# A decode step of gated attention and a squared-ReLU FFN: FFN, wo and q products placed ahead of the V-products in TensorE's order, and one maximum placed ahead of another pair's V-products

## The chip, the core and the metric

The kernel runs on one core of a Trainium2 chip. The metric is the device time of one execution in microseconds (us), and less is better. Five engines take part, each with an instruction stream of its own that it works through strictly in order: TensorE (PE in the profile, with its weight loads as PEld), VectorE (DVE), ScalarE (ACT), GpSimd (POOL) and SyncE (SP). SP computes nothing here; it issues nearly all the loads from HBM, and an issue that has to wait holds up the issues behind it. All loads of SP go out on one DMA queue (q1).

## What is computed

One token of decoding for a batch of two. The result mixes an attention block over a cache of 4096 positions (16 heads of 256) with an FFN, with a gate per batch row:

```python
def _A_ref(x, k_cache, v_cache, wq, wo):
    q = (x @ wq).reshape(B, Sq, H, Dh).transpose(0, 2, 1, 3)
    scores = jnp.einsum("bhqd,bhkd->bhqk", q, k_cache) * (Dh ** -0.5)
    p = _softmax(scores, axis=-1)
    o = jnp.einsum("bhqk,bhkd->bhqd", p, v_cache)
    return o.transpose(0, 2, 1, 3).reshape(B, Sq, H * Dh) @ wo

def _B_ref(x, w1, b1, w2, b2):
    h = jnp.einsum("bsd,df->bsf", x, w1) + b1
    r = jnp.where(h > 0, h, 0)
    return jnp.einsum("bsf,fd->bsd", r * r, w2) + b2

g = _sigmoid((x * gate_w).sum(-1, keepdims=True))
return g * _A_ref(x, ...) + (1 - g) * _B_ref(x, ...)
```

x is [2, 1, 448], K and V are [2, 16, 4096, 256] each, wq is [448, 4096], wo is [4096, 448], w1 is [448, 1792] and w2 is [1792, 448], all float32.

## The kernel before

The 32 pairs of a batch row b and a head h are numbered i = 2h + b. Each pair has one K tile and one V tile of 128 partitions x 8192 floats (4096 KB). In the tile names of the program k0_3 is the K tile of b = 0, h = 3, which is pair 6; the profile leaves the numbers out and writes k and v.

**The ring.** All big loads share one pool of five such tiles (`RING`, line 54; `slot`, line 68): wq, w1, w2 in two parts, four groups of wo, and every K and V. A load may be issued once the tile that stood in its buffer was read for the last time. SP issues in the order of the code: in iteration i of the loop at line 351 the K of pair i+1, then the V of pair i, then what else falls due there: w1 at i = 2, the first half of w2 at i = 4, a group of wo at every h % 4 = 2 with b = 1 (i = 5, 13, 21, 29), the second half of w2 at the last pair. At i = 29 (`last - 2`) the K of pairs 30 and 31 are issued together; the last V comes in three pieces.

**The order.** `tc.manual_schedule()` (line 66) keeps each engine's instructions in the order of the code. For pair i the loop runs:

- `maximum(i)` (line 281): DVE takes the maximum m of a row of scores, PE transposes and spreads it (mt, line 285);
- `times_q(i+1, ...)` (line 268): DVE multiplies the next pair's K by q in place, in two pieces around `softmax(i)`, whose first step nb (line 291, DVE) reads mt, and whose exponential p is on ACT (line 294);
- for b = 1, `sums` (PE, line 299) and `norm` (DVE, line 304 onward);
- `values(i)` (line 311): PE multiplies p with V, 16 products of two passes each into po_buf;
- behind it on PE, when it falls due: the spreading of q for later heads (`make_q`, line 218), `turn(h)` (line 320: ACT copies po_buf, PE transposes it to ot, ACT writes oT), the wo products (`project`, line 333), the FFN's first layer with its transposition (`ffn_hidden`, line 232, i = 3) and the first seven w2 products (line 397, i = 5);
- the rest of `times_q(i+1)` and the row sums of pair i+1 (`row_sums`, line 275), both DVE; and at i = 3, behind these, `ffn_square` (line 251), DVE's bias, ReLU and square, which reads the transposed hidden layer pt out of PSUM.

So a V that lands late holds up, on PE, all that stands behind `values(i)`, the next pair's mt among it. At the end, `late` (line 338) adds the last w2 and wo products into fin, ACT copies it to y4 and two small DMAs write the result.

Of the kernel before, what the change touches and what calls it, by code (L numbers as in the profile page):

```python
# [8 lines left out]
F32 = mybir.dt.float32  # L9
# [7 lines left out]
def kernel(  # L17
# [14 lines left out]
    nc = tc.nc  # L32
    P = 128
    B, H, S, DH = k_cache.shape
    D = x.shape[-1]
    F = w1.shape[1]
# [6 lines left out]
    J = 32  # L43
    NCH = NK // J
    HG = 4
    NG = H // HG
# [5 lines left out]
    QH = QB // DH  # L52
    DQ = D // 4
    RING = 5
    WH = FC // 2
    LEAD = 4
    LEAD2 = 16
# [56 lines left out]
    def load_wo(g):  # L114
        t = slot(f"wo{g}")
        tv = t[:, :HG * NJ * D].rearrange("p (h k) -> p h k", h=HG)
        nc.sync.dma_start(tv, wo_v[:, g * HG:(g + 1) * HG, :])
        wo_sb[g] = tv.rearrange("p h (j n) -> p h j n", j=NJ)
# [99 lines left out]
    def make_q(b, n):  # L218

        a, gq = divmod(n, 4)  # L220
        r = 32 * gq + b
        pq = ps.tile([P, 512], F32, name=f"pq{b}_{n}", tag="pq")
        nc.tensor.matmul(pq, ident[:, r:r + 1].to_broadcast([P, P]), qs[:, a, :], start=True, stop=True)  # L223
        t = work.tile([P, QB], F32, name=f"q{b}_{n}", tag=f"q{b}")
        nc.scalar.activation(t, pq, AF.Copy)  # L225
        for k in range(QH):
            q_sb[b, n * QH + k] = t[:, k * DH:(k + 1) * DH]


    hT = const.tile([P, FC, B], F32, name="hT")  # L230

    def ffn_hidden():
        h_sb = const.tile([B, F], F32, name="h_sb")
        ph = ps.tile([P, 512], F32, name="ph", tag="pq")
        for c in range(CF + 1):
            for n in range(FB):
                if c < CF:
                    lt, rhs = xT[:, c, :], w1_t[c][:, n * D:(n + 1) * D]
                else:
                    half, m = divmod(n, FB // 2)  # L240
                    lt, rhs = xT[:, CF + half, :], w1_t[c][:, m * D:(m + 1) * D]
                nc.tensor.matmul(ph[32 * n:32 * n + B, :D], lt, rhs, start=(c == 0), stop=(c == CF))  # L242
        for n in range(FB):
            nc.scalar.activation(h_sb[:, n * D:(n + 1) * D], ph[32 * n:32 * n + B, :D], AF.Copy)  # L244
        hv = h_sb.rearrange("b (p c) -> b c p", c=FC)
        pt = ps.tile([P, FC, B], F32, name="pt", tag="sm")
        for c in range(FC):
            nc.tensor.matmul(pt[:, c, :], hv[:, c, :], ident[:B, :B], start=True, stop=True)  # L248
        return pt
# [31 lines left out]
    def maximum(i):  # L281
        m = work.tile([P, 1], F32, name=f"m{i}", tag="m")
        nc.vector.tensor_reduce(m, s_t[i], axis=AX.X, op=ALU.max)  # L283
        mt = ps.tile([P, 512], F32, name=f"mt{i}", tag="sm")
        nc.tensor.matmul(mt[:, :P], m.to_broadcast([P, P]), ident, start=True, stop=True)  # L285
        return mt
# [10 lines left out]
    def sums(h):  # L297
        sm = ps.tile([P, 512], F32, name=f"sum{h}", tag="sm")
        nc.tensor.matmul(sm[:, :B], ones_pp, rs_t[h], start=True, stop=True)  # L299
        return sm  # L300

    def norm(h, sm):
        rc = work.tile([P, B], F32, name=f"rc{h}", tag="rc")
        nc.vector.reciprocal(rc, sm[:, :B])
        nc.vector.tensor_mul(rc, rc, gP[:, 0, :])
        rl = work.tile([P, B, 2], F32, name=f"rl{h}", tag="rl")
        nc.vector.tensor_tensor(rl, m4.rearrange("p (b s) -> p b s", s=2), rc.unsqueeze(2).to_broadcast([P, B, 2]),
                                op=ALU.mult)
        rl_t[h] = rl

    def values(i, vt):
        b, h = pairs[i]
        po = po_bufs[h % 2]
        for m in range(NK // 2):
            r = 32 * (m % 4)
            j = 2 * m
            nc.tensor.matmul(po[r:r + 4, :], p4[b][:, m, :], vt[j // J][:, j % J:j % J + 2, :].rearrange("p j d -> p (j d)"),  # L317
                             start=(b == 0 and m < 4), stop=(b == B - 1 and m >= NK // 2 - 4))
# [14 lines left out]
    def project(h):  # L333
        for j in range(NJ):
            nc.tensor.matmul(acc[:, :D], oT[h][:, j, :], wo_sb[h // HG][:, h % HG, j, :], start=False,  # L335
                             stop=(h == H - 2 and j == NJ - 1))

    def late(lt, rhs, start=False, stop=False):
        for k in range(4):
            nc.tensor.matmul(fin[32 * k:32 * k + B, :DQ], lt, rhs[:, k * DQ:(k + 1) * DQ], start=start, stop=stop)  # L340
# [6 lines left out]
    for n in range(NCH):  # L347
        times_q(0, n * J, (n + 1) * J)
        row_sums(0, n * J, (n + 1) * J)
    sm = None  # L350
    for i, (b, h) in enumerate(pairs):

        for n in (range(i + 1, i + 2) if i < last - 2 else range(i + 1, last + 1) if i == last - 2 else ()):
            kts[n] = load_kv(k_cache, n, "k")
        vt = load_kv(v_cache, i, "v", (J // 2, 3 * J // 4) if i == last else ())
        if i == 2:
            load_w1()
        if i == 4:
            load_w2_early()
        if h % HG == HG - 2 and b == B - 1:  # L360
            load_wo(h // HG)
        if i == last:
            load_w2_late()

        mt = maximum(i)
        if i < last:
            times_q(i + 1, 0, LEAD)
        softmax(i, mt)
        if i < last:
            times_q(i + 1, LEAD, LEAD2)  # L370
        if b == B - 1:
            norm(h, sums(h))
        if i == last - 1:

            for hh in range(H - HG, H - 1):
                project(hh)
            ya = const.tile([B, D], F32, name="ya")
            nc.scalar.activation(ya, acc[:, :D], AF.Copy)
            late(ident[:B, :B], ya, start=True)
        values(i, vt)  # L380
        if b == 0 and h % QH == QH - 1 and h + 1 < H:
            make_q(0, (h + 1) // QH)
        if b == 1 and h % QH == QH - 1 and h + 1 < H:
            make_q(1, (h + 1) // QH)
        if b == B - 1:
            turn(h)
        if h % HG == HG - 1 and h < H - 1:
            if b == 0:
                for hh in range(h - HG + 1, h):
                    project(hh)  # L390
            else:
                project(h)
        if i == 3:
            pt = ffn_hidden()
        if i == 5:
            for c in range(WH):
                nc.tensor.matmul(acc[:, :D], hT[:, c, :], w2_sb[c], start=False, stop=False)
        if i < last:
            times_q(i + 1, LEAD2, J)
            row_sums(i + 1, 0, J)  # L400
            for n in range(1, NCH):
                times_q(i + 1, n * J, (n + 1) * J)
                row_sums(i + 1, n * J, (n + 1) * J)
        if i == 3:
            ffn_square(pt)

    for c in range(WH, FC - 2):
# [37 lines left out]
```

## Time and profile before

| | |
|---|---|
| median of three runs | 697.7 us (696.03 to 698.03) |
| the profiled execution | 695.98 us, its span 694.2 us |
| VectorE busy | 583.4 us (84%), 260 instructions |
| ScalarE busy | 41.3 us (6%) |
| GpSimd busy | 0.7 us |
| granted TensorE clock, mean | 0.683 |

The span runs from the first to the last instruction of the program; 1.8 us of the execution lie around it. Busy time is a mean over stages, and the stages of this kernel differ only at three places: the start (about 30 us until the first K has landed), pairs 3 to 7, where the FFN is worked in, and the end from pair 29 on. In between, the same pattern of two loads to a pair repeats. The rows that carry the argument stand in the prediction.

### The profile page before, as it was taken

The page shows a single profiled execution, that of the slowest core. Times are in us where ns is not written, and L with a number is a line of the kernel's source. Part 1 is how long each engine was busy: PE and PEld are TensorE (multiplying, and loading weights), DVE is VectorE, ACT ScalarE, POOL GpSimd, SP SyncE. Part 2 cuts the span into 40 slices and gives each one's busy share as a digit, 9 for nine tenths or more (in the row PEclk, how much of TensorE's full clock was granted, in tenths as well). Part 3 has the DMA queues.
Part 4 walks back from the last instruction along what each step waited for, and adds up shares of the span by engine and source line. Part 5 has one row for each costly group of instructions (what it writes and reads, how often), then busy time and mean ns, then how long its engine had stood idle before and what let it go on. Part 6 is the DMA issues. An engine that isn't in the chain of part 4 may idle for free.

```text
span 694.2 us, 3854 instructions
## 1 busy us (share of the span) xinstructions
PE 296.8 (43%) x1570; PEld 89.3 (13%) x1570; DVE 583.4 (84%) x260; ACT 41.3 (6%) x123; POOL 0.7 (0%) x6
## 2 busy tenths in 40 slices
PE   4312443737165344432276344332465433344265
PEld 1000110502011010100111011010111001011012
DVE  2299988299969998999689999999689999999781
ACT  0200000100000000000000000000000000000000
POOL 0000000000000000000000000000000000000000
PEclk9756665757576666766577755766568665665597
DMA  9999999998899999999999999999999999999992
GB/s 369 448 423 437 434 427 425 426 441 363 334 448 426 425 446 424 427 436 425 424 440 431 426 440 427 431 430 417 438 433 434 429 432 430 436 427 430 429 416 116
DMA packets 13100, 289.79 MB, mean 417 GB/s; under 512 B 1430, under 2 KB 1436, under 8 KB 3868
## 3 DMA queue, kind: packets, MB, share of 16 engines
q1 hardware_dynamic: 12920, 289.54, 97.4%
q8 instruction: 12, 0.20, 0.1%
q10 hardware_dynamic: 164, 0.02, 0.0%
q14 instruction: 4, 0.03, 0.0%
HBM read 289.56 MB, written 0.00 MB: 417 GB/s over the span
## 4 chain that ended last, share of the span: by engine, by line
DMA 57%; DVE 31%; PE 9%; ACT 1%; issue 1%; SPq 0%; DVEq 0%; ACTq 0%
DMA k<-in_A_k_cache_dram 32%; DMA v<-in_A_v_cache_dram 25%; DVE s L279 15%; DVE k L273 15%; PE po_buf L317 5%; PE pt L248 1%; PE ot L329 1%; PE acc L335 1%; PE pq L223 1%; ACT o L323 0%; PE mt L285 0%; PE ph L242 0%; DVE nb L291 0%; ACT q L225 0%; ACT h_sb L244 0%
## 5 line engine op out<-in xcount | busy, mean ns | idle before, releaser
L273 DVE TENSOR_TENSOR k<-k,q 128x3072 f32<-128x3072 f32 (+3 forms) x94 | 286.0, 3057 | 60.1 <-DMA k<-in_A_k_cache_dram 60.0
L317 PE MATMUL po_buf<-v,p 128*4 128x512 f32 x1024 | 180.8, 870 | 234.5 <-DMA v<-in_A_v_cache_dram 232.5
L279 DVE TENSOR_REDUCE s<-k 128x32 f32<-128x8192 f32 x32 | 277.9, 8686 | 2.2
L317 PEld LDWEIGHTS po_buf<-v,p 128*4 128x4 f32 x1024 | 30.1, 109 | 359.5 <-issue 253.2
L285 PE MATMUL mt<-ident,m 128*128 128x128 f32 x64 | 19.5, 395 | 96.6 <-DVE m L283 96.5
L294 ACT ACTIVATE p<-s,nb 128x32 f32<-128x32 f32 x32 | 10.4, 324 | 288.8 <-DVE nb L291 288.8
L285 PEld LDWEIGHTS mt<-ident,m 128*128 128x128 f32 x64 | 12.4, 241 | 115.5 <-issue 92.6
L335 PE MATMUL acc<-wo,oT 128*2 128x448 f32 x60 | 24.3, 550 | 0.8 <-ACT oT L331 0.8
L329 PE MATMUL ot<-rl,o 128*128 128x2 f32 x128 | 17.7, 260 | 14.8 <-ACT o L323 14.8
L299 PE MATMUL sum<-rs,ones_pp 128*128 128x2 f32 x32 | 8.4, 331 | 34.8 <-ACT p L294 34.8
L225 ACT ACTIVATE q<-pq 128x512 f32<-128x512 f32 x16 | 9.6, 597 | 200.9 <-PE pq L223 200.9
L291 DVE TENSOR_REDUCE nb<-mt 128x1 f32<-128x128 f32 x32 | 9.1, 285 | 13.2 <-PE mt L285 13.1
L329 PEld LDWEIGHTS ot<-rl,o 128*128 128x128 f32 x128 | 16.3, 196 | 29.0 <-ACT o L323 29.0
L223 PE MATMUL pq<-qs,ident 128*128 128x512 f32 x32 | 17.7, 641 | 0.0
L323 ACT ACTIVATE o<-po_buf 128x512 f32<-128x512 f32 x16 | 9.5, 595 | 112.0 <-PE po_buf L317 112.0
L299 PEld LDWEIGHTS sum<-rs,ones_pp 128*128 128x128 f32 x32 | 7.0, 273 | 38.4 <-ACT p L294 38.4
L253 DVE TENSOR_TENSOR hb<-pt,b1T 128x28 f32<-128x28 f32 x1 | 0.2, 188 | 13.5 <-PE pt L248 13.5
L248 PE MATMUL pt<-ident,h_sb 2*128 2x2 f32 x28 | 7.0, 378 | 2.3 <-ACT h_sb L244 2.3
L248 PEld LDWEIGHTS pt<-ident,h_sb 2*128 2x128 f32 x28 | 6.9, 336 | 3.1 <-ACT h_sb L244 3.1
L283 DVE TENSOR_REDUCE m<-s 128x1 f32<-128x32 f32 x32 | 5.9, 186 | 1.1
L223 PEld LDWEIGHTS pq<-qs,ident 128*128 128x128 f32 x32 | 4.8, 187 | 14.6 <-issue 13.7
L335 PEld LDWEIGHTS acc<-wo,oT 128*2 128x2 f32 x60 | 4.5, 84 | 16.8 <-issue 15.7
(58 smaller groups left out, 61.2 us busy)
## 6 DMA issues: line engine op xcount, KB each, us to landing
k<-in_A_k_cache_dram SPq DMA_DIRECT2D x32, 4096.0 KB, 25.0
v<-in_A_v_cache_dram SPq DMA_DIRECT2D x31, 4096.0 KB, 30.8
wo<-in_A_wo_dram SPq DMA_DIRECT2D x4, 1792.0 KB, 34.2
wqa<-in_A_wq_dram SPq DMA_DIRECT2D x1, 4096.0 KB, 12.4
wqb<-in_A_wq_dram SPq DMA_DIRECT2D x1, 2048.0 KB, 16.9
v<-in_A_v_cache_dram SPq DMA_DIRECT2D x1, 2048.0 KB, 20.3
v<-in_A_v_cache_dram SPq DMA_DIRECT2D x2, 1024.0 KB, 22.4
w<-in_B_w_dram SPq DMA_DIRECT2D x1, 1792.0 KB, 28.4
```

The lines of the kernel that those rows point to most:

```text
L223: nc.tensor.matmul(pq, ident[:, r:r + 1].to_broadcast([P, P]), qs[:, a, :], start=True, stop=True)
L225: nc.scalar.activation(t, pq, AF.Copy)
L248: nc.tensor.matmul(pt[:, c, :], hv[:, c, :], ident[:B, :B], start=True, stop=True)
L273: nc.vector.tensor_tensor(kt, kt, q_sb[b, h].unsqueeze(1).to_broadcast([P, e - a, DH]), op=ALU.mult)
L279: nc.vector.tensor_reduce(s_t[i][:, n * J + a:n * J + e], kts[i][n][:, a:e, :], axis=AX.X, op=ALU.add)
L285: nc.tensor.matmul(mt[:, :P], m.to_broadcast([P, P]), ident, start=True, stop=True)
L294: nc.scalar.activation(p4[b][:, :, 2 * b:2 * b + 2], s_t[i].rearrange("p (m s) -> p m s", s=2), AF.Exp, bias=nb, accum_out=rs_t[h][:, b:b ...
L299: nc.tensor.matmul(sm[:, :B], ones_pp, rs_t[h], start=True, stop=True)
L317: nc.tensor.matmul(po[r:r + 4, :], p4[b][:, m, :], vt[j // J][:, j % J:j % J + 2, :].rearrange("p j d -> p (j d)"), start=(b == 0 and m < ...
L323: nc.scalar.activation(o, po, AF.Copy)
L329: nc.tensor.matmul(ptv[:, j, :], ov[:, s, j, :], rl_t[h][:, :, s], start=(s == 0), stop=(s == 1))
L335: nc.tensor.matmul(acc[:, :D], oT[h][:, j, :], wo_sb[h // HG][:, h % HG, j, :], start=False, stop=(h == H - 2 and j == NJ - 1))
```

## The change

The change removes no product and no byte; it places work differently.

1. `ffn_hidden` is cut in three. The products with w1 stay at i = 3, but stand ahead of `values(3)`; the transposition (`ffn_turn`) is at i = 4 ahead of `values(4)`; `ffn_square` on DVE follows the row sums at the end of i = 4 instead of i = 3.
2. The seven w2 products of i = 5, and each `make_q`, stand ahead of `values` of the same pair.
3. The wo groups 0 to 2 are loaded two pairs later (i = 7, 15, 23), and their eight products all stand ahead of `values` at i = 8, 16, 24.
4. At i = 29 the row sums and the maximum of pair 30 are written ahead of `values(29)`; on DVE that changes no order, on PE mt of pair 30 stands ahead.

```diff
--- before.py
+++ after.py
@@ -229,8 +229,9 @@
 
     hT = const.tile([P, FC, B], F32, name="hT")
 
+    h_sb = const.tile([B, F], F32, name="h_sb")
+
     def ffn_hidden():
-        h_sb = const.tile([B, F], F32, name="h_sb")
         ph = ps.tile([P, 512], F32, name="ph", tag="pq")
         for c in range(CF + 1):
             for n in range(FB):
@@ -242,6 +243,8 @@
                 nc.tensor.matmul(ph[32 * n:32 * n + B, :D], lt, rhs, start=(c == 0), stop=(c == CF))
         for n in range(FB):
             nc.scalar.activation(h_sb[:, n * D:(n + 1) * D], ph[32 * n:32 * n + B, :D], AF.Copy)
+
+    def ffn_turn():
         hv = h_sb.rearrange("b (p c) -> b c p", c=FC)
         pt = ps.tile([P, FC, B], F32, name="pt", tag="sm")
         for c in range(FC):
@@ -347,7 +350,14 @@
     for n in range(NCH):
         times_q(0, n * J, (n + 1) * J)
         row_sums(0, n * J, (n + 1) * J)
-    sm = None
+
+    def rest(i):
+        times_q(i, LEAD2, J)
+        row_sums(i, 0, J)
+        for n in range(1, NCH):
+            times_q(i, n * J, (n + 1) * J)
+            row_sums(i, n * J, (n + 1) * J)
+
     for i, (b, h) in enumerate(pairs):
 
         for n in (range(i + 1, i + 2) if i < last - 2 else range(i + 1, last + 1) if i == last - 2 else ()):
@@ -357,12 +367,14 @@
             load_w1()
         if i == 4:
             load_w2_early()
-        if h % HG == HG - 2 and b == B - 1:
-            load_wo(h // HG)
+        grp = h // HG
+        if b == B - 1 and h == (H - 2 if grp == NG - 1 else grp * HG + HG - 1):
+            load_wo(grp)
         if i == last:
             load_w2_late()
 
-        mt = maximum(i)
+        if i != last - 1:
+            mt = maximum(i)
         if i < last:
             times_q(i + 1, 0, LEAD)
         softmax(i, mt)
@@ -370,6 +382,20 @@
             times_q(i + 1, LEAD, LEAD2)
         if b == B - 1:
             norm(h, sums(h))
+
+
+        if h % QH == QH - 1 and h + 1 < H:
+            make_q(b, (h + 1) // QH)
+        if h % HG == 0 and b == 0 and h > 0:
+            for hh in range(h - HG, h):
+                project(hh)
+        if i == 3:
+            ffn_hidden()
+        if i == 4:
+            pt = ffn_turn()
+        if i == 5:
+            for c in range(WH):
+                nc.tensor.matmul(acc[:, :D], hT[:, c, :], w2_sb[c], start=False, stop=False)
         if i == last - 1:
 
             for hh in range(H - HG, H - 1):
@@ -377,31 +403,16 @@
             ya = const.tile([B, D], F32, name="ya")
             nc.scalar.activation(ya, acc[:, :D], AF.Copy)
             late(ident[:B, :B], ya, start=True)
+
+        if i == last - 2:
+            rest(i + 1)
+            mt = maximum(i + 1)
         values(i, vt)
-        if b == 0 and h % QH == QH - 1 and h + 1 < H:
-            make_q(0, (h + 1) // QH)
-        if b == 1 and h % QH == QH - 1 and h + 1 < H:
-            make_q(1, (h + 1) // QH)
         if b == B - 1:
             turn(h)
-        if h % HG == HG - 1 and h < H - 1:
-            if b == 0:
-                for hh in range(h - HG + 1, h):
-                    project(hh)
-            else:
-                project(h)
-        if i == 3:
-            pt = ffn_hidden()
-        if i == 5:
-            for c in range(WH):
-                nc.tensor.matmul(acc[:, :D], hT[:, c, :], w2_sb[c], start=False, stop=False)
-        if i < last:
-            times_q(i + 1, LEAD2, J)
-            row_sums(i + 1, 0, J)
-            for n in range(1, NCH):
-                times_q(i + 1, n * J, (n + 1) * J)
-                row_sums(i + 1, n * J, (n + 1) * J)
-        if i == 3:
+        if i < last and i != last - 2:
+            rest(i + 1)
+        if i == 4:
             ffn_square(pt)
 
     for c in range(WH, FC - 2):
```

The first place is PE's order from the V-products of pair 3 on (v1_1; po_buf holds two heads' sums), with ph the FFN's first layer, pt its transposition, w2 the products with the first half of w2, and ot, mt and sum as above. Before:

```order
L317 MATMUL po_buf1_94<-v1_1_0_306,p4_1_101 4x512 x16
L223 MATMUL pq1_1_340<-qs_133,ident_85 128x512
L329 MATMUL ot1_346<-rl1_322,o1_344 128x2 x4
L242 MATMUL ph_354<-w1_267,xT_114 2x448 x16
L248 MATMUL pt_375<-ident_85,h_sb_353 128x2 x14
L285 MATMUL mt4_406<-ident_85,m4_404 128x128
L317 MATMUL po_buf0_92<-v0_2_0_400,p4_0_99 4x512 x16
L285 MATMUL mt5_441<-ident_85,m5_439 128x128
L299 MATMUL sum2_448<-rs2_411,ones_pp_90 128x2
L317 MATMUL po_buf0_92<-v1_2_0_435,p4_1_101 4x512 x16
L329 MATMUL ot2_473<-rl2_453,o2_471 128x2 x4
L397 MATMUL acc_96<-w2_0_402,hT_134 2x448 x7
```

And now:

```order
L223 MATMUL pq1_1_325<-qs_133,ident_85 128x512
L243 MATMUL ph_329<-w1_268,xT_114 2x448 x16
L320 MATMUL po_buf1_94<-v1_1_0_307,p4_1_101 4x512 x16
L332 MATMUL ot1_368<-rl1_323,o1_366 128x2 x4
L288 MATMUL mt4_386<-ident_85,m4_384 128x128
L251 MATMUL pt_394<-ident_85,h_sb_135 128x2 x14
L320 MATMUL po_buf0_92<-v0_2_0_380,p4_0_99 4x512 x16
L288 MATMUL mt5_439<-ident_85,m5_437 128x128
L302 MATMUL sum2_446<-rs2_391,ones_pp_90 128x2
L398 MATMUL acc_96<-w2_0_382,hT_134 2x448 x7
L320 MATMUL po_buf0_92<-v1_2_0_435,p4_1_101 4x512 x16
L332 MATMUL ot2_478<-rl2_451,o2_476 128x2 x4
```

pq and ph now precede the V-products of pair 3, pt (14 transpositions) those of pair 4, and w2 those of pair 5 (v1_2). The row sum of the softmax (sum2) stays ahead of w2.

The second place is SP's order of loads from the first half of w2 on. What a load waits for stands behind it: an engine's name is the one that last read the buffer, and a DMAHW name is an earlier load's semaphore (DMAHW1 to DMAHW4 are here K of pair 4, V of pair 3, K of pair 5 and V of pair 4; DMAHW6, and 7 and 0 in the first rows, are w1, and from the V of pair 6 on DMAHW6 is K of pair 6). Before:

```order
L104 DMA w2_0_402<-in_B_w2_dram 128x3136 [waits DMAHW1_49,DVE_49]
L128 DMA k0_3_0_433<-in_A_k_cache_dram 128x8192 [waits DMAHW6_49,DMAHW2_49,PE_49]
L128 DMA v1_2_0_435<-in_A_v_cache_dram 128x8192 [waits DMAHW7_49,DMAHW0_49,PE_49]
L117 DMA wo0_437<-in_A_wo_dram 128x4x896 [waits DMAHW4_49,PE_49]
L128 DMA k1_3_0_490<-in_A_k_cache_dram 128x8192 [waits DMAHW3_49,DVE_49]
L128 DMA v0_3_0_492<-in_A_v_cache_dram 128x8192 [waits DMAHW6_49,DVE_49]
L128 DMA k0_4_0_533<-in_A_k_cache_dram 128x8192 [waits DMAHW7_49,PE_49]
L128 DMA v1_3_0_535<-in_A_v_cache_dram 128x8192 [waits DMAHW5_49,PE_49]
```

And now:

```order
L104 DMA w2_0_382<-in_B_w2_dram 128x3136 [waits DMAHW6_49,DMAHW7_49,DMAHW0_49,PE_49]
L128 DMA k0_3_0_433<-in_A_k_cache_dram 128x8192 [waits DMAHW1_49,DVE_49]
L128 DMA v1_2_0_435<-in_A_v_cache_dram 128x8192 [waits DMAHW2_49,PE_49]
L128 DMA k1_3_0_488<-in_A_k_cache_dram 128x8192 [waits DMAHW3_49,DVE_49]
L128 DMA v0_3_0_490<-in_A_v_cache_dram 128x8192 [waits DMAHW4_49,PE_49]
L128 DMA k0_4_0_525<-in_A_k_cache_dram 128x8192 [waits DMAHW5_49,PE_49]
L128 DMA v1_3_0_527<-in_A_v_cache_dram 128x8192 [waits DMAHW7_49,PE_49]
L117 DMA wo0_529<-in_A_wo_dram 128x4x896 [waits DMAHW6_49,DVE_49]
```

The w2 load takes the buffer of w1, freed by PE, instead of that of a K, freed by DVE. The V of pair 6 (v0_3) took the buffer of K of pair 6, which DVE's row sums free; it now takes that of V of pair 4, which PE frees. The wo load stands behind the V of pair 7 instead of ahead of the K of pair 7.

The third place is PE's order at pairs 29 and 30 (v1_14 is the V of pair 29). Before:

```order
L285 MATMUL mt29_1500<-ident_85,m29_1498 128x128
L299 MATMUL sum14_1507<-rs14_1468,ones_pp_90 128x2
L317 MATMUL po_buf0_92<-v1_14_0_1494,p4_1_101 4x512 x16
L329 MATMUL ot14_1532<-rl14_1512,o14_1530 128x2 x4
L285 MATMUL mt30_1546<-ident_85,m30_1544 128x128
L335 MATMUL acc_96<-wo3_1496,oT12_1363 2x448 x2
```

And now:

```order
L288 MATMUL mt29_1500<-ident_85,m29_1498 128x128
L302 MATMUL sum14_1507<-rs14_1468,ones_pp_90 128x2
L288 MATMUL mt30_1519<-ident_85,m30_1517 128x128
L320 MATMUL po_buf0_92<-v1_14_0_1494,p4_1_101 4x512 x16
L332 MATMUL ot14_1539<-rl14_1512,o14_1537 128x2 x4
L338 MATMUL acc_96<-wo3_1496,oT12_1363 2x448 x2
```

mt of pair 30 has moved from behind the V-products and the turn of pair 29 to ahead of both.

## The prediction

> **What bounds the kernel now.** First the page: the lines of the DMA engines in 40 slices of the span, and the line of SP's queue.
>
> ```profile
> PE 296.8 (43%) x1570; PEld 89.3 (13%) x1570; DVE 583.4 (84%) x260; ACT 41.3 (6%) x123; POOL 0.7 (0%) x6
> DMA  9999999998899999999999999999999999999992
> GB/s 369 448 423 437 434 427 425 426 441 363 334 448 426 425 446 424 427 436 425 424 440 431 426 440 427 431 430 417 438 433 434 429 432 430 436 427 430 429 416 116
> ...
> q1 hardware_dynamic: 12920, 289.54, 97.4%
> ```
>
> The loads bound it: DVE is busy 84%, PE 43%, but SP's queue 97.4%, at a level rate. Only the first slice, slices 10 and 11 and the last fall off. So I ask the windows for the rate and for the dip (last two columns: DMA share, GB/s).
>
> ```profile
> 30.00:140.00 110.00, 42.30 (x221) 17.15 (x221) 90.55 (x38) 6.43 (x18) 0.00 (x0) 0.64 1.00 430
> 140.00:210.00 70.00, 35.06 (x156) 8.92 (x160) 63.99 (x29) 3.02 (x11) 0.00 (x0) 0.70 0.93 394
> 173.00:174.00 1.00, 0.00 (x0) 0.00 (x0) 1.00 (x1) 0.00 (x0) 0.00 (x0) 1.00 0.00 0
> 200.00:650.00 450.00, 183.51 (x921) 51.27 (x920) 411.31 (x172) 23.93 (x79) 0.00 (x0) 0.66 1.00 431
> 320.00:330.00 10.00, 4.32 (x24) 0.80 (x28) 9.83 (x6) 0.00 (x0) 0.00 (x0) 0.50 0.97 403
> ```
>
> The stream runs at 430 GB/s before the dip and 431 after it, so no order of work makes a K or V tile (4096 KB, 4.19 MB) cheaper than 4.19 / 0.430 = 9.75 us. What can be won is time in which the queue is empty, and what follows the last load. Around 173 us the queue is empty. The timeline there, with SP's issues, shows why.
>
> ```profile
> 125.86 0.37 SPq L128 DMA_DIRECT2D k<-in_A_k_cache_dram  x1
> 131.84 6.97 PE L248 MATMUL pt<-ident,h_sb 2*128 2x2 f32 x28 [2.30 <-ACT h_sb L244]
> 138.85 0.19 DVE L253 TENSOR_TENSOR hb<-pt,b1T 128x28 f32<-128x28 f32 x1 [13.45 <-PE pt L248]
> 141.68 5.78 PE L317 MATMUL po_buf<-v,p 128*4 128x512 f32 x32 [0.98 <-ACT p L294]
> 157.47 0.34 SPq L128 DMA_DIRECT2D k<-in_A_k_cache_dram  x1
> 157.48 0.19 DVE L283 TENSOR_REDUCE m<-s 128x1 f32<-128x32 f32 x1
> 159.57 0.58 PE L299 MATMUL sum<-rs,ones_pp 128*128 128x2 f32 x2 [1.00 <-ACT p L294]
> 166.96 5.42 PE L397 MATMUL acc<-w,hT 128*2 128x448 f32 x14
> 167.19 8.69 DVE L279 TENSOR_REDUCE s<-k 128x32 f32<-128x8192 f32 x1
> 175.90 0.33 SPq L128 DMA_DIRECT2D v<-in_A_v_cache_dram  x1
> ```
>
> DVE stands 13.45 us at L253, because pt comes on PE only behind the V-products of pair 3. DVE's row sums of pair 6 so end at 167.19 + 8.69 = 175.88, and the V load that takes that K's buffer goes out at 175.90, 18.43 us after the load before it. By then everything issued has landed.
>
> The end, from the maximum of pair 30 on, and the landing times from the page's list of DMA issues (KB each, us from issue to landing):
>
> ```profile
> 654.06 1.28 SPq L128 DMA_DIRECT2D v<-in_A_v_cache_dram  x3
> 654.07 0.19 DVE L283 TENSOR_REDUCE m<-s 128x1 f32<-128x32 f32 x1
> 654.17 1.21 DVE L273 TENSOR_TENSOR k<-k,q 128x1024 f32<-128x1024 f32 x1
> 660.32 0.33 SPq L108 DMA_DIRECT2D w<-in_B_w_dram  x1
> 661.94 0.47 PE L285 MATMUL mt<-ident,m 128*128 128x128 f32 x2
> 662.45 0.29 DVE L291 TENSOR_REDUCE nb<-mt 128x1 f32<-128x128 f32 x1 [7.06 <-PE mt L285]
> 669.46 3.62 PE L317 MATMUL po_buf<-v,p 128*4 128x512 f32 x32 [1.46 <-DMA v<-in_A_v_cache_dram]
> 679.16 0.18 DVE L283 TENSOR_REDUCE m<-s 128x1 f32<-128x32 f32 x1
> 679.49 0.77 PE L285 MATMUL mt<-ident,m 128*128 128x128 f32 x2 [6.41 <-DVE m L283]
> 681.67 5.44 PE L317 MATMUL po_buf<-v,p 128*4 128x512 f32 x32
> 688.87 1.14 PE L340 MATMUL fin<-w,hT 128*2 128x112 f32 x40
> 690.85 0.26 ACT L414 ACTIVATE y<-fin 128x112 f32<-128x112 f32 x1 [1.69 <-PE fin L340]
> ...
> k<-in_A_k_cache_dram SPq DMA_DIRECT2D x32, 4096.0 KB, 25.0
> ...
> v<-in_A_v_cache_dram SPq DMA_DIRECT2D x1, 2048.0 KB, 20.3
> v<-in_A_v_cache_dram SPq DMA_DIRECT2D x2, 1024.0 KB, 22.4
> w<-in_B_w_dram SPq DMA_DIRECT2D x1, 1120.0 KB, 21.7
> ```
>
> Here the loads do not set the end. nb of pair 30 waits 7.06 us for mt, which stands on PE behind the V-products of pair 29; from it DVE runs without a pause to the maximum of pair 31, and the last V-products start at 681.67. The last V quarter, issued by about 654.9, landed by 654.9 + 22.4 = 677.3.
>
> **Term 1, the dip: 5.3 us go.** At 430 GB/s the 70 us from 140 to 210 lack (430 - 394) / 430 x 70 = 5.9 us. A wo group (small pieces) lies in this stretch; the window 320 to 330, with another wo, lacks (430 - 403) / 430 x 10 = 0.6 us, and that stays. 5.9 - 0.6 = 5.3 us. Bounds: 3 us (only the seconds at zero) and 5.9 us.
>
> Does the queue stay full then? DVE no longer waits at L253: `ffn_square` runs a pair later, when pt has long been there, so the row sums of pair 5 end not at 157.48 but 13.45 us sooner, at 144.0, and the K of pair 7 goes out then. The V of pair 6 waits no more for DVE's row sums but for the V-products of pair 4. Before, these ended at 141.68 + 5.78 = 147.5; now pt (7.0 us) stands ahead of them, but mt of pair 4 comes 13.45 us sooner too (the row sums of pair 4 end at 138.85 - 13.45 = 125.4), so they are no later. That V so goes out at 147.5 at the latest, 28 us ahead of 175.90. Next in line, the K of pair 8 waits for w2. w2 stands behind the sum of pair 5, and that behind the landing of pair 6's K, about 125.86 + 25.0 = 150.9; from maximum to sum it is 159.57 - 157.48 = 2.1 us, then 0.6 for the sum and 5.4 for w2: 150.9 + 8.1 = 159 us. The queue then still holds the K of pair 7 and the V of pair 6, two tiles or 19.5 us. The V of pair 7 follows pair 5's V-products a few us later. So each comes more than a tile ahead of need, and no dip takes this one's place.
>
> **Term 2, the end: 6.8 us go.** All times here are in the clock of the old profile; term 1 moves them alike. mt of pair 30 runs at 654.4 on an idle PE and takes 0.77 us, to 655.2. nb then waits for nothing and starts when the product ends, 655.4, not 662.45. DVE keeps 7.06 us: the maximum of pair 31 ends at 679.34 - 7.06 = 672.3. What is late next is PE: the V-products of pair 30 start when that V lands, 669.46, and last to 673.1. mt of pair 31 stands behind them, which gives back 0.8 us. From its start to the V-products of pair 31 it is 681.67 - 679.49 = 2.2 us: 675.3. Then 16 products: 3.62 us as for pair 30, or 5.44 as before; the first half of the V has been there since 654.06 + 20.3 = 674.4, the last quarter since 677.3. End at 678.9 or 680.7. From there to fin 688.87 - (681.67 + 5.44) = 1.8 us: 680.7 or 682.5. But the fin pass needs the w load of 660.32, landed at 660.32 + 21.7 = 682.0. So fin starts at 682.0 or 682.5, and y follows 690.85 - 688.87 = 2.0 us later: 684.0 or 684.5, not 690.85. I take the first, since the row nearest in place and in idle time (1.46 us) is the 3.62: 6.8 us. The very last w piece (448 KB, 1.1 us of stream) lands at 683.1, just ahead of its pass. Bounds: 6.85 above; 4.9 below, if fin's 2.0 us take twice that.
>
> The granted clock bears on those bounds: 5.44 us followed an idle PE, 3.62 a busy one. The Trainium skill, TensorE: Matmul & The Clock Gate, section Part 1, says that TensorE falls to half rate after an idle window of about 3.4 us and comes back after as long a busy one. By that rule fin, after a wait of 1.3 us, keeps its rate and the end is worth 6.8 us; with a rate halved at every wait it would be 4.9. The rows agree with the rule: 1.46 us of idle time before 3.62, 6.41 before 5.44.
>
> **What is only moved.** The groups of instructions give its size on PE.
>
> ```profile
> L335 PE MATMUL acc<-wo,oT 128*2 128x448 f32 x60 | 24.3, 550 | 0.8 <-ACT oT L331 0.8
> L223 PE MATMUL pq<-qs,ident 128*128 128x512 f32 x32 | 17.7, 641 | 0.0
> L242 PE MATMUL ph<-w,xT 128*2 128x448 f32 x32 | 3.2, 539 | 0.0
> ```
>
> 48 of 60 wo passes (19.4 us), 28 of 32 pq passes (15.5), ph 3.2, pt 7.0 and w2 5.4 make 50.5 us now ahead of V-products. I cost them at nothing. Their cover is the wait for V: V of a pair lands one tile, 9.75 us, behind the K of the next, at which the pair's maximum is about due. The heaviest pieces are w2 with sum (the 8.1 us above), pt with mt (7.7) and 16 wo passes with mt (6.5 + 0.8). Each fits. What exceeds it delays mt of the next pair, which DVE wants 18.4 us after the last. The extra instructions: none; `ffn_square`'s four (0.19 us each) only move. On SP's queue each wo load moves behind four K and V issues; it then stands two tiles ahead of the V of the pair whose V-products wait behind its products, so it lands before they could start anyway.
>
> **Sum.** 5.3 + 6.8 = 12.1 us. The profiled execution took 695.98 us (span 694.2 and 1.8 around it), 1.7 below the median of 697.7. So 683.9 for an execution like that one, 685.6 for the median.
>
> **Rivals.** *A dry queue elsewhere* takes the place of the one removed; only term 2 is left: 697.7 - 6.8 = 690.9 us. For it: five buffers, of which the FFN's weights take one. Against it: the two tiles of cover.
>
> *The end does not pay*, because another wait stands where nb's stood; only term 1: 692.4 us. For it: the fin pass is already at its load. Against it: no row between 655.4 and 672.3 waits for anything but DVE.
>
> *The stream itself is the limit on average*, and gives back after a pause what it missed: then term 1 is nothing, again 690.9 us. Against it: the 110 us before the dip and the 450 after it run at 430 and 431 alike. The Trainium skill, DMA: Bandwidth & Descriptors, section Specifications, gives a memory limit of about 358 GB/s per core and a fabric ceiling of 435. By 358 the 289.54 MB alone would take 809 us, by 435 they take 666; the trace's 694.2 refutes the first and fits the second.
>
> *Slower: PE gets onto the path.* Place: the moved work at pairs 3 to 5 and at every fourth head, if V has landed before it is done. Price at most its 50.5 us: 697.7 - 12.1 + 50.5 = 736 us. From about a quarter of it (12.1 / 50.5) on the change is slower than before. For it: the margin of w2 is only 9.75 - 8.1 = 1.7 us. Against it: DVE's 18.4 us to a pair leave PE, with mt, pt and V-products 0.8 + 7.0 + 5.8 = 13.6 us, 4.8 us more.
>
> **How the numbers follow.** The forecast has 0.80; the first two rivals 0.06 each, the stream 0.02, no effect at all 0.03, slower 0.03. Bounds of the forecast: 3 + 4.9 = 7.9 and 5.9 + 6.85 = 12.75 us; with the runs' spread (1.7 below the median, 0.3 above) 683.2 to 690.1. I widen this to 683.0 to 690.2, which leaves the rivals out, no more than 2 in 10. About 0.3% (2.1 us) is what a measurement can tell from no change: faster 0.94, same 0.03, slower 0.03.
>
> **What would show it.** Right: no second with 0 GB/s near 173 us and slices 10 and 11 near 430; no wait at ffn_square; nb of pair 30 without its 7.06 us and mt of pair 31 released by PE's own products; the last fin passes released by a w load; a span near 682. Wrong: a new stretch under 400 GB/s; values of pair 4, 5 or 8 released by PE's own work instead of V; DVE waiting for mt anywhere by microseconds; a last landing less than 5 us earlier.

## The result, and the profile after

| | before | after |
|---|---|---|
| median | 697.0 us (696.03 to 698.03, 4 runs) | 686.4 us (684.5 to 686.92, 4 runs) |
| ratio | 1 | 0.984 [0.982, 0.987] |
| the profiled execution | 695.98 us, span 694.2 | 686.92 us, span 685.1 |
| VectorE busy | 583.4 us | 583.3 us |

10.6 us less between the medians, 9.1 between the profiled executions, with the same work on VectorE: what went is waiting. The page of the changed kernel first, its line of GB/s in 40 slices and its line of SP's queue.

```profile
GB/s 371 445 436 430 428 432 426 417 442 428 429 428 438 432 429 430 429 430 432 428 418 449 428 429 431 430 428 430 438 431 425 429 430 430 434 434 431 413 430 192
...
q1 hardware_dynamic: 12920, 289.54, 98.7%
```

Slices 10 and 11 (363 and 334 before) now read 428 and 429, each slice being a fortieth of the span. The windows of the changed kernel (the last two columns are DMA share and GB/s) give the same for the stretch from 140 to 210 us and for the second that stood at zero.

```profile
140.00:210.00 70.00, 36.17 (x168) 10.64 (x161) 59.98 (x30) 3.86 (x12) 0.00 (x0) 0.70 1.01 430
173.00:174.00 1.00, 0.00 (x0) 0.00 (x0) 1.00 (x1) 0.00 (x0) 0.00 (x0) 0.50 0.84 360
200.00:650.00 450.00, 193.25 (x923) 53.18 (x915) 405.77 (x168) 22.98 (x76) 0.00 (x0) 0.66 1.00 431
```

So the stretch went from 394 to 430 GB/s. Next, what DVE waits for in all, as the view of waits lists it for the changed kernel (us in total, times, the longest).

```profile
DVE k L276 <- DMA k<-in_A_k_cache_dram: 74.7, 28, 20.4
DVE nb L294 <- PE mt L288: 1.3, 1, 1.3
```

Before, the same view had 60.0 us of waits for K, and these for pt and mt:

```profile
DVE hb L253 <- PE pt L248: 13.5, 1, 13.5
DVE nb L291 <- PE mt L285: 13.1, 6, 7.1
```

Of these 26.6 us for PE, 1.3 us at one nb are left (the same view has 1.0 us more at the last sum and 2.3 at the start, much as before). Nearly all the rest of DVE's waiting is for loads, as it should be in a kernel that loads bound. The timeline of the changed kernel around the former dip shows it in place.

```profile
126.78 6.97 PE L251 MATMUL pt<-ident,h_sb 2*128 2x2 f32 x28
136.75 5.78 PE L320 MATMUL po_buf<-v,p 128*4 128x512 f32 x32 [3.00 <-DMA v<-in_A_v_cache_dram]
144.64 0.18 DVE L256 TENSOR_TENSOR hb<-pt,b1T 128x28 f32<-128x28 f32 x1
144.75 0.33 SPq L128 DMA_DIRECT2D k<-in_A_k_cache_dram  x1
145.17 0.38 SPq L128 DMA_DIRECT2D v<-in_A_v_cache_dram  x1
160.82 0.33 SPq L128 DMA_DIRECT2D k<-in_A_k_cache_dram  x1
```

pt lies inside the wait for V of pair 4, of which 3.00 us are left; L256 waits for nothing; the V of pair 6 goes out at 145.17, not at 175.90. The end of the changed kernel, in the same view:

```profile
650.91 0.28 DVE L294 TENSOR_REDUCE nb<-mt 128x1 f32<-128x128 f32 x1
665.03 3.62 PE L320 MATMUL po_buf<-v,p 128*4 128x512 f32 x32 [2.01 <-DMA v<-in_A_v_cache_dram]
669.10 0.29 DVE L294 TENSOR_REDUCE nb<-mt 128x1 f32<-128x128 f32 x1 [1.29 <-PE mt L288]
672.44 1.04 PE L320 MATMUL po_buf<-v,p 128*4 128x512 f32 x8 [0.28 <-DMA v<-in_A_v_cache_dram]
674.92 1.04 PE L320 MATMUL po_buf<-v,p 128*4 128x512 f32 x8 [1.44 <-DMA v<-in_A_v_cache_dram]
676.68 1.58 PE L332 MATMUL ot<-rl,o 128*128 128x2 f32 x8 [0.72 <-ACT o L326]
678.20 2.05 PE L343 MATMUL fin<-w,hT 128*2 128x112 f32 x40
681.80 0.26 ACT L425 ACTIVATE y<-fin 128x112 f32<-128x112 f32 x1 [3.33 <-PE fin L343]
```

nb of pair 30 no longer waits, and the last four products (x8, two passes each) wait for the last quarter of V. From fin to y it is 681.80 - 678.20 = 3.6 us, where it was 2.0. The windows of the changed kernel say why: TensorE's clock (third column from the end) falls to half.

```profile
676.00:678.00 2.00, 1.32 (x8) 1.32 (x8) 0.00 (x0) 0.60 (x1) 0.00 (x0) 0.76 0.25 101
678.00:680.00 2.00, 2.00 (x42) 1.61 (x45) 0.00 (x0) 0.17 (x1) 0.00 (x0) 0.50 0.00 2
```

### The profile page after: what moved, and what is told of

Its sections match the earlier page's. It is cut to its first block, busy times and chain, and to the rows that moved or that the text cites. A ratio compares the mean times of both kernels' runs of the same rounds, so it can differ in the third digit from the quotient of the medians.

```text
span 685.1 us, 3851 instructions
## 1 busy us (share of the span) xinstructions
PE 307.8 (45%) x1570; PEld 93.5 (14%) x1570; DVE 583.3 (85%) x260; ACT 41.2 (6%) x123; POOL 0.7 (0%) x6
## 4 chain that ended last, share of the span: by engine, by line
DMA 61%; DVE 35%; PE 3%; issue 0%; SPq 0%; ACT 0%; DVEq 0%; ACTq 0%
DMA k<-in_A_k_cache_dram 57%; DVE k L276 17%; DVE s L282 17%; DMA v<-in_A_v_cache_dram 4%; PE acc L398 1%; PE acc L338 1%; PE fin L343 1%; DVE nb L294 0%; PE ot L332 0%; DVE m L286 0%; DVE rc L308 0%; DVE rl L310 0%; PE po_buf L320 0%; SPq L128 0%; DVE rc L307 0%
## 5 line engine op out<-in xcount | busy, mean ns | idle before, releaser
L320 PE MATMUL po_buf<-v,p 128*4 128x512 f32 x1024 | 173.3, 834 | 186.8 <-DMA v<-in_A_v_cache_dram 185.7
L223 PE MATMUL pq<-qs,ident 128*128 128x512 f32 x32 | 29.3, 1020 | 0.0
L338 PE MATMUL acc<-wo,oT 128*2 128x448 f32 x60 | 25.7, 586 | 0.0
L223 PEld LDWEIGHTS pq<-qs,ident 128*128 128x128 f32 x32 | 8.0, 305 | 1.3 <-ACT qs L214 0.9
L398 PE MATMUL acc<-w,hT 128*2 128x448 f32 x14 | 8.2, 759 | 0.0
## 6 DMA issues: line engine op xcount, KB each, us to landing
v<-in_A_v_cache_dram SPq DMA_DIRECT2D x2, 1024.0 KB, 22.3
```

## The experiments

Each was timed beside the kernel before; ratios are to it, with their 95% intervals. e1 to e4 ran on one chip, e5 to e8 on a second, e9 and e10 on a third; the kernel before had medians of 696.5, 696.5 and 696.4 us there.

| kernel | median, us | ratio |
|---|---|---|
| e1_no_max | 693.0 (691.91 to 693.75) | 0.9944 [0.9932, 0.9957] |
| e2_only_max | 693.0 (692.52 to 693.38) | 0.9946 [0.9934, 0.9959] |
| e3_square_late | 696.0 (694.65 to 696.95) | 0.9987 [0.9978, 0.9996] |
| e4_ffn_max | 685.9 (684.56 to 686.15) | 0.9847 [0.9834, 0.9861] |
| e5_after | 685.5 (684.59 to 686.59) | 0.9839 [0.9821, 0.9857] |
| e6_fill | 685.7 (684.73 to 685.84) | 0.9839 [0.9823, 0.9854] |
| e7_turn_twice | 686.8 (684.78 to 687.18) | 0.9851 [0.9833, 0.9870] |
| e8_two_parts | 684.5 (684.42 to 686.78) | 0.9824 [0.9809, 0.9838] |
| e9_fill3 | 684.7 (684.50 to 684.81) | 0.9829 [0.9816, 0.9842] |
| e10_two_parts_fill3 | 684.5 (684.29 to 684.83) | 0.9827 [0.9813, 0.9840] |

**Each term alone.** e1 is the changed kernel with the maximum of pair 30 back behind the V-products of pair 29; e2 is the kernel before with nothing but that maximum moved.

```diff
 e1, against after
-        if i != last - 1:
-            mt = maximum(i)
+        mt = maximum(i)
...
-        if i == last - 2:
-            rest(i + 1)
-            mt = maximum(i + 1)
         values(i, vt)
```

> The changed kernel with its last part undone: mt of pair 30 stands again behind the V-products and the turn of pair 29. Theory (two gains that add up, 4.5 us from the dip near 173 us by the shift of the landings between the two profiles, the rest at the end): 692.5 us against 697.0 before (ratio 0.9935), no second at 0 GB/s near 173, no wait of DVE at the FFN's bias, and nb of pair 30 waiting about 7 us for mt again. Rival A (closing the dip is worth what the bytes lacked, 5.3 to 5.9 us): 691.1 to 691.7. Rival B (the dip is all of the gain and the end pays nothing): 686.4, like the changed kernel.

> The kernel before with this one part alone: row sums and maximum of pair 30 written ahead of the V-products of pair 29. Theory (the end is a gain by itself, then bounded by the landing of the last V quarter and by the rate of the fin passes): 690.2 to 692.4 us (6.8 to 4.6 less than 697.0), the dip near 173 us still there at 0 GB/s, nb of pair 30 without its 7 us, the last V-products released by V. Rival (the end is bound by the loads already): 697, with the wait moved to a load.

Alone, the terms are worth 3.4 and 3.5 us by the medians (696.5 for the kernel before in that batch), together 10.6. e1 came near its 692.5; e2 missed its range of 690.2 to 692.4. The terms do not add up, and the timelines say why. e1 first:

```profile
650.66 6.11 PE L320 MATMUL po_buf<-v,p 128*4 128x512 f32 x32 [16.93 <-DMA v<-in_A_v_cache_dram]
658.97 0.29 DVE L294 TENSOR_REDUCE nb<-mt 128x1 f32<-128x128 f32 x1 [8.18 <-PE mt L288]
664.87 3.62 PE L320 MATMUL po_buf<-v,p 128*4 128x512 f32 x32 [0.34 <-DMA v<-in_A_v_cache_dram]
678.20 6.00 PE L320 MATMUL po_buf<-v,p 128*4 128x512 f32 x32
687.93 0.26 ACT L421 ACTIVATE y<-fin 128x112 f32<-128x112 f32 x1 [1.70 <-PE fin L343]
```

In e1 the dip is gone (430 GB/s from 140 to 210 us) and V of pair 30 starts its products at 664.87 instead of 669.46, 4.6 us sooner. But nb of pair 30 waits 8.18 us, since the V-products of pair 29 took 6.11 us in this execution (5.00 in the timeline of the kernel before), and the last ones took 6.00 instead of 5.44. y so comes 690.85 - 687.93 = 2.9 us sooner: 4.6 less 1.11 and 0.56. And e2:

```profile
680.70 1.04 PE L317 MATMUL po_buf<-v,p 128*4 128x512 f32 x8 [2.38 <-DMA v<-in_A_v_cache_dram]
682.46 1.87 PE L329 MATMUL ot<-rl,o 128*128 128x2 f32 x8 [0.72 <-ACT o L323]
684.26 2.05 PE L340 MATMUL fin<-w,hT 128*2 128x112 f32 x40
687.87 0.26 ACT L422 ACTIVATE y<-fin 128x112 f32<-128x112 f32 x1 [3.33 <-PE fin L340]
```

Here nb of pair 30 waits for nothing, and the last quarter of V sets the end, 680.70; behind it ot and fin run at half clock and y follows 7.2 us later. With the maximum moved, a stream that is earlier pulls the whole end forward: from e2 to the changed kernel that quarter's products move from 680.70 to 674.92, 5.8 us, and the medians by 6.6. (That is more than the 4.4 to 4.8 us by which the V-products of pair 30 move; why the last quarter gains another us is not shown.)

**The square alone.** e3 is the kernel before with only DVE's square moved from pair 3 to pair 4.

```diff
 e3, against before
-        if i == 3:
+        if i == 4:
             ffn_square(pt)
```

> The kernel before with one line changed: the FFN's bias, ReLU and square on DVE run at the end of pair 4's iteration instead of pair 3's; nothing moves on PE. Theory (the dip comes from DVE's 13.45 us alone): the dip goes, 692.5 us as in the run without the maximum; SP's loads of pairs 6 and 7 go out some 13 us earlier. Rival (the dip comes from PE's order, w1 and w2 being released only behind V-products): the dip stays or moves, 695 to 697 us.

This theory fell: 696.0 us, 0.5 below the kernel before. The timeline of e3:

```profile
131.97 6.97 PE L248 MATMUL pt<-ident,h_sb 2*128 2x2 f32 x28 [2.29 <-ACT h_sb L244]
138.87 0.80 PE L285 MATMUL mt<-ident,m 128*128 128x128 f32 x2
139.70 0.29 DVE L291 TENSOR_REDUCE nb<-mt 128x1 f32<-128x128 f32 x1 [11.83 <-PE mt L285]
175.38 0.33 SPq L128 DMA_DIRECT2D v<-in_A_v_cache_dram  x1
```

The wait of 13.45 us moved to the next DVE instruction that needs PE: nb of pair 4, 11.83 us, because mt of pair 4 stands behind ph and pt on PE. The V of pair 6 still goes out at 175.38. What makes the dip is PE's block of FFN work behind the V-products of pair 3, not the DVE instruction that the profile names; e8 below is the other half of the proof. One thing no run separates: moving this block also gives the V of pair 6 another buffer (that of the V of pair 4 instead of that of the K of pair 6). An estimate says that DVE's relief alone would do: 13.45 us sooner than 175.90 that V goes out at 162.5, and in the kernel before the loads ran at over 300 GB/s until 171 us.

**Without the moved wo and q work.** e4 is the changed kernel with the wo loads, the wo products and `make_q` back at their old places behind the V-products.

```diff
 e4, against after
...
-        if b == B - 1 and h == (H - 2 if grp == NG - 1 else grp * HG + HG - 1):
+        if h % HG == HG - 2 and b == B - 1:
...
-        if h % QH == QH - 1 and h + 1 < H:
-            make_q(b, (h + 1) // QH)
-        if h % HG == 0 and b == 0 and h > 0:
-            for hh in range(h - HG, h):
-                project(hh)
...
         values(i, vt)
+        if h % QH == QH - 1 and h + 1 < H:
+            make_q(b, (h + 1) // QH)
...
```

> The changed kernel with two parts undone: the wo loads at pairs 5, 13, 21 and their products, and the products for q, stand again where they stood before, behind the V-products. Theory (these were hidden on both sides): 686.4 us, within 2 us of the changed kernel. Rival (their place on PE gates mt, and with it DVE and the loads): 689 us or more, with DVE waiting for mt at the fourth heads.

685.9 us, as the changed kernel (686.4, and 685.5 in e5): this part of the change is worth nothing that can be measured. The end of its chain of waits (start, us, what):

```profile
656.23 21.20 DMA w<-in_B_w_dram
677.47 1.95 PE fin L343 x72
```

In this execution (684.56 us) fin waits for the w load, and takes 1.95 us at full clock. The last V quarter started its products at 674.55, y came at 679.45: 4.9 us, against 6.9 in the profile of the changed kernel.

**Two parts, and more work on PE.** e8 puts the transposition right behind the products with w1 at pair 3, and the square at the end of i = 3; e7 runs the 14 transpositions at pair 4 twice.

```diff
 e8, against after
         if i == 3:
             ffn_hidden()
-        if i == 4:
             pt = ffn_turn()
...
-        if i == 4:
+        if i == 3:
             ffn_square(pt)
```

```diff
 e7, against after
         if i == 4:
             pt = ffn_turn()
+            hv = h_sb.rearrange("b (p c) -> b c p", c=FC)
+            for c in range(FC):
+                nc.tensor.matmul(pt[:, c, :], hv[:, c, :], ident[:B, :B], start=True, stop=True)
```

> The first layer in two parts instead of three: the transposition stands right behind the products with w1 at pair 3, both ahead of the V-products of pair 3, and the square follows the row sums at the end of i = 3. Theory (the dip came of FFN work between the V-products of pair 3 and mt of pair 4, and ends once it stands ahead of V-products): no dip, about 686.4 us, nb of pair 4 waiting 5 us at most. Rival (the third part is what removes the dip, since at pair 3 ph and pt together outlast the wait for V): the dip is back, 691 to 693 us.

> Adds work only: the 14 transpositions of the hidden layer at pair 4 run twice, 7 us more on PE ahead of the V-products of pair 4. Theory (what stands ahead of a V-product hides in the wait for V, and an overshoot of a few us is covered by DVE's row sums and by two tiles in the queue): same as the unaltered kernel beside it, within 1 us, and 140 to 210 us still at about 430 GB/s. Rival (the margin at pair 4 is used up, PE comes onto the path): 4 to 7 us more, DVE waiting for mt of pair 5, or the dip near 173 us back.

The timeline of e8, and its window from 140 to 210 us:

```profile
133.77 0.29 DVE L294 TENSOR_REDUCE nb<-mt 128x1 f32<-128x128 f32 x1 [5.95 <-PE mt L288]
150.41 0.33 SPq L128 DMA_DIRECT2D k<-in_A_k_cache_dram  x1
```

```profile
140.00:210.00 70.00, 36.94 (x165) 10.69 (x158) 64.97 (x27) 3.98 (x12) 0.00 (x0) 0.70 1.01 430
```

nb of pair 4 waits 5.95 us, a little over the 5 us forecast, and the K of pair 7 goes out 5.7 us later than in the changed kernel, yet the queue does not run dry. Together with e3 this settles the dip: with the square at pair 3 as in the kernel before, and only PE's FFN work in another place, it is gone. Two parts are enough, and the third is worth nothing that can be measured (e10 and e9 below, 684.5 and 684.7 us, differ in it alone). The timeline of e7:

```profile
133.46 6.95 PE L398 MATMUL pt<-ident,h_sb 2*128 2x2 f32 x28
140.34 5.38 PE L320 MATMUL po_buf<-v,p 128*4 128x512 f32 x32
145.65 0.49 PE L288 MATMUL mt<-ident,m 128*128 128x128 f32 x2
145.79 0.33 SPq L128 DMA_DIRECT2D v<-in_A_v_cache_dram  x1
```

The V-products of pair 4 start 3.6 us later and now wait for PE, not for V, but mt of pair 5 is no later (145.63 in the changed kernel) and the V of pair 6 goes out 0.6 us later. 140 to 210 us still read 430 GB/s. Seven more us of PE work ahead of V-products cost no more than some tenths of a us here: the executions took 684.78 and 686.64 to 687.18 us, those of the changed kernel (with e5) 684.50 to 684.77 and 686.13 to 686.92. The medians of e5, e7 and e8 differ by up to 2.3 us for another reason, which is next.

**The clock of the end.** The five kernels that end alike and carry no small products (the changed one, e4, e5, e7, e8) have 22 executions: 9 took 684.4 to 684.8 us, 13 took 685.9 to 687.2, and none lies between. Their profiles divide in the same way: the one execution of 684.56 us ran its end at full clock, those of 686.28 to 687.18 us (the changed kernel, e5, e7, e8) ran fin at half clock.

What differs between them lies further ahead. In the four profiles that end at half clock, the clock reads 1.00 from 660 to 676 us, TensorE waits 1.44 or 1.45 us for the last V quarter and 0.72 us for o, and the clock is down to 0.50 by 678 us. e4 has this row and, as the second, its clock from 666 to 668 us:

```profile
664.69 5.31 PE L320 MATMUL po_buf<-v,p 128*4 128x512 f32 x32 [1.11 <-DMA v<-in_A_v_cache_dram]
666.00:668.00 2.00, 2.00 (x16) 0.50 0.96 406
```

There the clock fell at 665 us and was back at 1.00 by 669. The V-products of pair 30 so took 5.31 us instead of 3.62, what follows them on PE came later, and ahead of the last quarter only 0.17 us of wait were left. So the full clock of e4's end goes with less idle time just before it, and not with the same waits.

The next runs put work into these waits. e5 is the changed kernel again; e6 puts seven small products ahead of the last four V-products and three behind them, e9 three and two, e10 is e8 with the small products of e9.

```diff
 e9, against after
+    def fill(n):
+        for _ in range(n):
+            nc.tensor.matmul(acc[:, :P], ident[:, :B], ident, start=True, stop=True)
...
+            if i == last and m == 11:
+                fill(3)
+            if i == last and m == 15:
+                fill(2)
```

> The changed kernel once more, unaltered, to stand beside the next three on the same chip. All theories: about 686.4 us, ratio about 0.984. What is read from it is its end: from the start of the V-products of the last quarter to the copy of y it was 6.9 us in the profile of the changed kernel (granted clock 0.5) and 4.9 us in that of the run with the old places of wo and q (clock 1.0). Theory that the clock of the end differs from execution to execution: either number, with spans 2 us apart.

> Adds work only: seven small products ahead of the last four V-products of pair 31 and three behind them, into a bank that is not read any more, so that TensorE is busy while it waits for the last V quarter and for o. Theory (the waits of 1.4 us and 0.7 us drop TensorE's clock, and the end pays 2 us for it): ot takes 1.1 us instead of 1.6, the last V quarter to y 4.9 us instead of 6.9, and the median comes out 1 to 2 us below the unaltered kernel beside it. Rival (the clock at the end is set earlier, or does not matter): same time within 0.5 us, or up to 1 us more, with ot at 1.6 us and fin to y at 3.5 us.

> As the run with seven and three small products, but three (0.7 us) ahead of the last four V-products and two behind them: less than the 1.44 us for which TensorE waits there, so that nothing is put off. Theory (the executions of the changed kernel that take 684.5 and those that take 686.5 us differ in the clock of the last 5 us, and a clock that falls there is a matter of TensorE's idle time just before): nearly all executions at 684.5 to 685 us, ot at 1.1 us and fin to y at 2.0 us. Rival (the clock at the end is drawn anew in each execution whatever PE does there): executions at both 684.5 and 686.5 us, as without the small products.

> The first layer in two parts, together with the three and two small products at the end. Theory: two parts are worth what three are, so the same as with the small products alone, 684.5 to 685 us in nearly all executions. Rival for the two parts: 0.5 us or more below it. Rival for the small products: executions at 686.5 us remain.

e6 missed its forecast of 1 to 2 us below e5: the small products outlasted the wait and put the last V-products off by about 1 us, so the median stayed (three executions at 685.7 to 685.8, one at 684.73). Its fin ran at full clock, but that proves little: in this execution, as in e4, the clock had fallen at 665 us already (the V-products of pair 30 took 5.25 us). e9 stays inside the wait. Its timeline, and a window of its clock:

```profile
672.97 0.82 PE L316 MATMUL acc<-ident 128*2 128x128 f32 x6
674.59 1.04 PE L324 MATMUL po_buf<-v,p 128*4 128x512 f32 x8 [0.80 <-DMA v<-in_A_v_cache_dram]
676.35 1.11 PE L340 MATMUL ot<-rl,o 128*128 128x2 f32 x8 [0.30 <-ACT o L334]
677.43 1.14 PE L351 MATMUL fin<-w,hT 128*2 128x112 f32 x40
679.41 0.26 ACT L433 ACTIVATE y<-fin 128x112 f32<-128x112 f32 x1 [1.74 <-PE fin L351]
```

```profile
678.00:680.00 2.00, 1.34 (x56) 1.07 (x47) 0.00 (x0) 0.26 (x1) 0.00 (x0) 1.00 0.00 0
```

All five executions of e9 and all four of e10 took 684.3 to 684.8 us: the second group is gone. In both profiles the V-products of pair 30 take 3.62 us, as in the four profiles that end at half clock, so they reach the end in the same way; the longest wait there is then 0.80 us, and the clock stays at 1.00. So work in PE's waits just ahead of the end keeps the clock up there, and a fallen clock costs some 2 us. Two limits: no kernel without small products ran on the chip of e9 and e10 except the kernel before, and the length of a wait is not all that counts, since 0.62 and 1.11 us of idle time just ahead of the V-products of pair 30 were enough in e4, and 0.62 and 2.01 were not in the changed kernel. e9 and e10 are 1.7 and 1.9 us below the changed kernel's 686.4; e8's median is as low, with one of its five executions at 686.78. The intervals of the ratios overlap, and what is plain is that the executions of e9 and e10 no longer spread.

## Why the prediction was right

686.4 us came for 685.6. The saving was forecast at 12.1 us and measured at 10.6 between the medians, 9.1 between the profiled executions; part of the nearness is luck, since the median of the kernel before stood at 697.7 with three executions and at 697.0 with four. By its own steps:

- *Bound and place of both terms.* Right. The queue was full once DVE no longer waited for PE; what stayed at the end is the landing of the last loads.
- *The working of the dip.* The K of pair 7 was to go out at 144.0 and went at 144.75, the V of pair 6 by 147.5 and went at 145.17, the K of pair 8 at 159 and went at 160.82. The naming of the cause was narrower than the truth: the text saw that pt is late because of PE's order, but put the repair on the square (it "runs a pair later"), and e3 shows that moving the square alone leaves an 11.83-us wait at the next instruction. The forecast held since the change moves the PE work too, which the prediction counted among the "only moved" work: ph and pt ahead of V-products are what removes the dip.
- *Term 1, 5.3 us.* Slightly too large. The V-products of pair 30 start 4.4 us sooner in the profile of the changed kernel (669.46 to 665.03), 4.8 in that of e9.
- *Term 2, 6.8 us.* Right in mechanism, and in size only where the clock stays up. In e9, y comes 690.85 - 679.41 = 11.44 us sooner, of which 4.75 belong to term 1: 6.7 for term 2. In the profiled execution of the changed kernel it is 9.05 - 4.4 = 4.6. The step that was mis-sized is "fin, after a wait of 1.3 us, keeps its rate", taken from the Trainium skill, TensorE: Matmul & The Clock Gate, Part 1, by which the clock falls after an idle window of about 3.4 us. Here the measurement differs from that rule: waits of 1.44 and 0.72 us were enough in all four profiles that have them without small products, and 4.6 us came, a little under the lower bound of 4.9.
- *The landing of the last V quarter at 677.3.* Too early by about 3 us: the row of 22.4 us stands for two pieces, and it is the earlier one's time (in the changed kernel the row says 22.3, and the chain of waits has 24.35 for the last piece). e2, whose last V is issued 0.34 us later than in the kernel before, starts that quarter's products at 680.70. By luck it changed little, because V quarter, o and ot reach fin at about the moment of the w load that the prediction took as the bound: 682.0 was forecast for fin, less 4.4 to 4.8 for term 1 that is 677.2 to 677.6, and it started at 677.43 in e9 and at 677.47 in e4, in the latter released by that load.
- *mt of pair 31 behind the V-products of pair 30.* 0.8 us forecast, 1.29 us of wait at nb; without effect, since V is later still.
- *Moved work at nothing.* Right, shown by e4 for wo and q, and by e7, which adds 7 us at pair 4.
- *The signs of being wrong.* Two of them came. The V-products of pair 5 are released by PE's own w2 products, not by V:

```profile
159.88 0.61 PE L320 MATMUL po_buf<-v,p 128*4 128x512 f32 x3
```

  They start without a wait, because the w2 products took some 8 us instead of 5.4; it cost nothing, since mt of pair 6 still waits 2.57 us for DVE. And the w load behind the last V lands 4.4 us earlier, not 5 (660.32 + 21.7 = 682.0 before, 655.66 + 21.9 = 677.6 now): that is the size of term 1 again.
- *Rivals.* A dry queue elsewhere: no slice between the second and the 39th reads under 413 GB/s; outside the dip the lowest was 416 before. The end does not pay (692.4): this is e1's time of 693.0, not the change's. The stream limited on average (690.9): refuted by 430 GB/s in the former dip and 431 behind it. PE on the path: refuted by e7 at pair 4; at other heads by e4, which takes that work back without a gain, and by DVE's waits for mt, 1.3 us in all.

## What to carry to other kernels

When an engine waits long at one instruction, look for what stands ahead of the releaser on the releasing engine, and move that: moving the waiting instruction hands its wait to the next one (11.8 of 13.5 us here). Two repairs of one chain are not worth the sum of what each is worth alone: 3.4 and 3.5 us apart, 10.6 together. With the maximum alone moved, the late loads set the end; with the dip alone closed, the wait for mt stood as before and slower V-products took 1.7 of the 4.6 us. Where the last loads set the end, keep TensorE busy through the waits there with work that ends before the load does.

## What the runs showed of the hardware

- *The clock falls on short waits.* With 1.44 and 0.72 us of idle time between 673.5 and 676.7 us, TensorE's clock fell from 1.00 to 0.50 about fin in all four profiles that have these waits without small products, and in e2 with waits of 2.38 and 0.72 us. With 0.80 and 0.30 us (e9, e10) or 0.17 and 0.72 us (e4) it stayed at 1.00 there. The Trainium skill, TensorE: Matmul & The Clock Gate, Part 1, says that the window is free-running, and that the moment of a change so differs from run to run; the two groups of times agree with this. That several short waits add up in one window is argued from e9, not measured by itself.
- *Work put into waits runs at a lower clock.* The products that spread q took 641 ns each before and take 1020 now, as the groups of instructions of the changed kernel show, and the w2 products 759 instead of 539. The clock from 169.2 to 171.2 us, where two of the q products stand, is 0.50; it was 1.00 from 194.6 to 195.7 us, where they stood before.

```profile
L223 PE MATMUL pq<-qs,ident 128*128 128x512 f32 x32 | 29.3, 1020 | 0.0
L398 PE MATMUL acc<-w,hT 128*2 128x448 f32 x14 | 8.2, 759 | 0.0
```

  Standing ahead of V-products they follow an idle PE, not a busy one. Here the wait for V covers it: PE's busy time rose from 296.8 to 307.8 us while the kernel got 10.6 us faster.
